# One more buffer for four attention tiles, and three small PSUM sums moved later, in a fused attention and two-layer kernel

## The chip, the cores and the metric

The kernel runs on one core of a Trainium2 chip. The metric is device microseconds of one execution. It was measured three times before the change; a fourth execution was taken with the hardware profiler, and all rows below are of that one.

## The reference

Attention over 4 batches, 8 heads, 576 positions, head size 64, with a causal mask and a bias from the running sums of `max(s, 0)`; the result, as 2304 tokens of 512, goes through two layers, `relu(x w_in)**2 w_out` and then `g w_out` with `g = h cos(h)`, `h = x w_in`, each with 2048 hidden columns.

```python
bias = -(cum[:, :, :, None] - cum[:, :, None, :])
scores = np.where(causal, -1e9, scale * q @ k.T + np.minimum(bias, 0.0))
attn = softmax(scores)
x = (attn @ v) as (2304, 512)
y = np.maximum(x @ w_in, 0.0) ** 2 @ w_out
h = y @ w2_in
out = (h * np.cos(h)) @ w2_out
```

## The kernel before, in words

Everything is written out by hand in one order for each engine; waits come from the tiles' dependencies. Work goes in two halves. In the first, attention for the next 256 tokens runs beside the first layer for the last 256: `step` (L1325) is called once for each attention job (at most 128 queries of one head), and each call also takes one or two slots of the first layer (`moe_slot`, L1285), 12 products each for one slice of 128 hidden columns, either into the slice (`g1`, L1148) or out of it (`g2`, L1189). In the second half only the second layer is left.

The first 16 heads run in a simple form, the other 80 units in a split form: a number is kept as a rounded part and a rest, and three products make one. For these, a call of `step` with job i does, in this order on TensorE: the first slot, the scores of job i (`emit_qk`, L539), further slots, the turning of a finished pair of heads (`turn`, L744), the product of job i-5 with v (`emit_pv`, L671). VectorE masks the scores of job i-1 (`emit_mask`, L573), rounds the weights p of job i-2 (`emit_split`, L629), evacuates finished heads (`evacuate`, L708), and makes the rests of the layer's slices (`grest`), of the turned x (`x_low`) and of the next head's q and k (`prep_low`, L406). ScalarE takes exponentials, squares and rounded parts (`prep_high`, L399, of q and k; `x_high`, L787, of x). SyncE issues nearly all DMAs in order: raw q and k of a head three ahead (`load_raw`, L239), v (`load_v`, L418) and the DMA transposes of p (`p_turn`, L624). GpSimd clears the ends of p's rows (L647) and issues the loads into k2.

The tiles in question lie in the pool `at` and rotate by tag. `raw` and `s` (the scores) have two buffers. `p` has two, and every third job takes the single buffer of tag `p3` instead, outside a stretch in which the weights are converted. `pt`, p turned, has three. Job i's `pt` is written at step i+2 and read at step i+5.

All small sums share one PSUM bank, `xps`: columns 0 to 255 take the turned x (L751), which `x_high` and `x_low` read; one column takes the sum of v's squares for a group of two heads (`v_sum`, L450), read by `v_scale` (L457, L461); 16 columns take the sums of the first layer's weight slices (`c_sums`, L834), read by `c_scales` (L841, L848).

There are 16 groups of v. `v_add` (L524) puts their parts on a list by step: square at the end of step t, sum at step t+1, scale at t+2. `v_late` runs at a step's end. A group with `v_wait` on the list has its sum at t+2, behind the first slot, and its scale at the end of the VectorE part of that step, behind the rounding of p, the slices' rests, the weights' conversion (`c_step`, L889) and `prep_low`:

```python
        slow = bool(vq) and any(f is v_wait for f, g in vq[0])
        if slow:
            v_sums()
```

In the kernel before only the third group has it. `c_step` squares the weights' slices one at a time (L861, ScalarE); `c_total` (L920) issues the sum for slices 0 to 11 and for 12 to 15 at the end of the step that squared the last of them. From the fourth block of tokens on the layer uses these scales.

Of the kernel before, what the change touches and what calls it, by code (L numbers as in the profile page):

```python
# [8 lines left out]
F32 = mybir.dt.float32  # L9
F32R = mybir.dt.float32r  # L10
F16 = mybir.dt.float16
# [7 lines left out]
B, H, S, D = 4, 8, 576, 64  # L19
# [4 lines left out]
NF = DFF // 128  # L24
# [18 lines left out]
SQ_A = 12  # L43
# [55 lines left out]
KQ = 832  # L99
# [32 lines left out]
def attention_moe_moe_kernel(  # L132
# [29 lines left out]
    at = at_stack.enter_context(tc.tile_pool(name="at", bufs=1, side="right"))  # L162
# [20 lines left out]
    wsc1, hs1, xm = sc1[:, 0:NF // 2], sc1[:, NF // 2:NF], sc1[:, NF:NF + 1]  # L183
    vsc = const.tile([128, B * H], F32, name="vsc")
    hd, vd, vown = {}, {}, {}
    cs = at.tile([128, S], F32, tag="s", bufs=2, name="cs")
    c8 = wp.tile([128, S], F32, tag=f"w{2 * NF - 8}", name="c8")
    nc.sync.dma_start(out=cs[0:32, 0:S], in_=s)
    wt, wst = {}, {}
# [34 lines left out]
    for x in range(H // 2):  # L224
        t = wp.tile([128, 2, 2 * BT], F32, tag=f"w{2 * NF - (2, 3, 4, 6)[x]}", name="early")
# [13 lines left out]
    def load_raw(n):  # L239
        nq, nl = _queries(heads[n]), heads[n][8]  # L240
        if n < H:
            return
        if n < EARLY:
            t = at.tile([128, KQ], F32, tag=("hi", "k2")[n % 2], bufs=2, name="early1")
            nc.sync.dma_start(out=t[0:64, 0:2 * BT], in_=qk[n, 0:64, 0:2 * BT])
            nc.sync.dma_start(out=t[64:66, 0:2 * BT], in_=c1_d[n - H])
            hd[n] = t
            return
        raw = at.tile([128, KQ], F32, tag="raw", bufs=2, name="raw")
        nc.sync.dma_start(out=raw[:, BT - nq:BT + nl], in_=qk[n, :, BT - nq:BT + nl])  # L250
        hd[n] = [None, None, raw]

# [114 lines left out]
    for x in range((XST + 1) // 2):  # L367
        t = wp.tile([128, 2, 512], F32, tag=f"w{2 * NF - 5 - x}", name="xst")
# [18 lines left out]
    lag1, wrest = [], []  # L387
# [136 lines left out]
    def v_add(gs, at, stored=True):  # L524

        for g, t in zip(gs, at):
            fs = []
            if g not in vs:
                fs, t = [(t, v_load)], t + 2
            late = g == gs[2]  # L530
            fs += [(t + 2, v_wait)] * late
            fs += [(t, v_square), (t + 1 + late, v_sum), (t + 2, v_scale), (t + 2, v_high), (t + 3, v_low)]
            for x, f in fs + [(t + 3, v_store)] * stored:
                vq.extend([] for _ in range(x + 1 - len(vq)))
                vq[x].append((f, g))
# [37 lines left out]
    def emit_mask(i):  # L573
        n, ti, q, r = jobs[i]
        j = jd[i]
        if _paired(heads[n]):
            if heads[n][2] % 2 == 0:
                return
            r = 128
        sb = at.tile([128, S + 2], F32, tag="s", bufs=2, name="sb")  # L580
        nb = sb[:, S:S + 2]
        for k, (p, c0, cn) in enumerate(j["ps"]):
            mo = 512 if _paired(heads[n]) and k else max(0, 384 - q + c0)
            nc.vector.tensor_tensor_reduce(  # L584
                out=sb[0:r, c0:c0 + cn], in0=p[0:r, 0:cn], in1=mask[0:r, mo:mo + cn],
                scale=-0.125, scalar=(3.0e38 if k == 0 else nb[0:r, 0:1]),
                op0=ALU.add, op1=ALU.min, accum_out=nb[0:r, k:k + 1],
            )
            yield
        j["sb"], j["nb"] = sb, nb[0:r, len(j["ps"]) - 1:len(j["ps"])]  # L590

    def p_tile(i):
        third = nw[2] >= 2 * NF and not wrest and i % 3 == 2 and (cdone[1] == 0 or 2 in w16 and 2 not in w32)
        return at.tile([128, 1280], F16, tag="p3" if third else "p", bufs=1 if third else 2, name="p")

    def emit_exp(i):
        n, ti, q, r = jobs[i]
# [31 lines left out]
    def emit_split(i):  # L629
        n, ti, q, r = jobs[i]  # L630
        j = jd[i]
        if _paired(heads[n]):
            if heads[n][2] % 2 == 0:
                return
            r = 128
        w, sb = j["w"], j["sb"]
        cw = 128 * ((w + 127) // 128)
        if n < EARLY:
            pp = j["ps"][0][0][:, BT:BT + cw]
            pt = at.tile([128, 640], F32, tag="pt", bufs=3, name="pt1")  # L640
            (nc.scalar.copy if ti else nc.vector.tensor_copy)(pt[:, 0:w], pp)
            j["pt"] = pt
            yield
            return
        p = p_tile(i)
        if cw > w:
            nc.gpsimd.memset(p[0:r, 0:2 * cw].rearrange("p (a c) -> p a c", a=2)[:, :, w:cw], 0.0)  # L647
        if 0 < cdone[1] and NF - 1 not in w16 and i % 2:
            nc.scalar.activation(out=p[0:r, 0:w], in_=sb[0:r, 0:w], func=ACTF.Copy, scale=PSC)  # L649
        else:  # L650
            nc.vector.tensor_scalar(  # L651
                out=p[0:r, 0:w], in0=sb[0:r, 0:w], scalar1=PSC, scalar2=None, op0=ALU.mult
            )
        yield
        nc.vector.scalar_tensor_tensor(  # L655
            out=p[0:r, cw:cw + w], in0=sb[0:r, 0:w], scalar=PSC, in1=p[0:r, 0:w],
            op0=ALU.mult, op1=ALU.subtract,
        )
        pt = at.tile([128, 1280], F16, tag="pt", bufs=3, name="pt")
        pt = pt[:, 0:2 * cw // 128 * r].rearrange("p (a r) -> p a r", r=r)  # L660
        turned.append((pt, p[0:r, 0:2 * cw]))
        if not last_block(i):
            p_turn()
        j["pt"] = pt
        if _paired(heads[n]):
            jd[i - 1]["pt"], j["pt"] = pt[:, :, 0:64], pt[:, :, 64:128]
        yield
# [161 lines left out]
    w16, cdone, csum, chigh, clow = {}, [0, 0, 0], [], [], []  # L829
# [57 lines left out]
    spare, w32 = [None], {}  # L887
# [29 lines left out]
            chigh.append((cdone[1], t))  # L917
            cdone[1] += 1

    def c_total():  # L920
        if cdone[0] == SQ_A and SQ_A not in csent:
            csent.append(SQ_A)
            c_sums(0, SQ_A)
        elif cdone[0] == NF and NF not in csent:
            csent.append(NF)
            c_sums(SQ_A, NF)

    csent = []
# [28 lines left out]
    nw = [2, 0, 0]  # L957
    stq = [(wp, 3)]
    p3 = [0]
# [314 lines left out]
    slots = []  # L1274
# [50 lines left out]
    def step(moe=0, bits=0, attn=True):  # L1325

        i = prog[0]
        held = len(xtq)
        prog[0] += attn
        if attn:  # L1330
            for j in stage(1, i - 2):
                emit_exp(j)
        x_high()
        if attn and job(i - 2):
            emit_turn(i - 2)
        if attn:
            heads_ahead(i, (next_, load_ext, 2))
        w_age()
        w_scales()
        n = moe_slot() if moe else None  # L1340
# [3 lines that stand above are left out]
        if attn:  # L1344
            heads_ahead(i, (nhigh, prep_high, 2))
        _weave(evacuate())
        y_evict()
        if not attn or g2done[0] < 2:
            rests()
        if xcq and xcq[-1][-1] and xcq[-1][0] == 1:  # L1350
            x_low()
        _weave(softmax_tail(i) if attn else None, w_step(bits), None if slow else v_early())
        x_low()
        rests()
        w_lows()
        if attn and job(i - 1) and jobs[i - 1][0] < EARLY:
            for j in stage(1, i - 1):
                emit_exp(j)
        act(n)
        if moe and slots and NF < slots[0][1] < (KC + 2) * NF:  # L1360
            c_step(slots[0][1])
        if attn:
            heads_ahead(i, (nlow, prep_low, 2))
        if slow:
            _weave(v_early())
        if not (attn and last_block(i)):
            y_store()
        if attn and job(i):
            emit_qk(i)
        if attn and last_block(i):  # L1370
            heads_ahead(i, (nraw, load_raw, 4))
        for _ in range(moe - 1):
            act(moe_slot())
            y_evict()
        w_sums()
        if attn:
            for j in stage(1, i - 1):
                emit_exp(j)
        behind = any(job(j) and _paired(heads[jobs[j][0]]) for j in (i - 6, i - 5))
        if attn and not behind:  # L1380
            values(i)
        turn(held if moe and i > last_job[0] + TURN_FROM else len(xtq))
        if not slow:
            v_sums()
        if attn:
            for j in stage(3, i - LAG[0]):
                if j > i - lag(j):
                    stages[3] -= 1
                    break
                emit_pv(j)  # L1390
        if attn and behind:
            values(i)
        if moe:
            c_total()
        p_turn()
        w_ahead()
        if attn:
            heads_ahead(i, (nraw, load_raw, 4))
        v_late()
        y_store()  # L1400
        if later and prog[0] >= later[0][0]:
            later.pop(0)[1]()
# [102 lines left out]
    while prog[0] < unit_done(0):  # L1505
        i = prog[0]
# [472 lines left out]
```

## Time and profile before

| | us |
|---|---|
| three runs | 964.85, 966.21, 966.48; median 966.21 |
| the profiled execution | 966.79 |
| its span, first to last instruction | 965.0 |
| TensorE busy | 933.0 (97%) |
| VectorE busy | 752.9 (78%) |
| ScalarE busy | 710.8 (74%) |
| GpSimd busy | 166.6 (17%) |
| granted TensorE clock | 1.00 of full speed all along |

TensorE is PE in the rows, its weight loads PEld, VectorE DVE, ScalarE ACT, GpSimd POOL; SPq is SyncE's queue. In a timeline row a bracket tells how long the engine was idle before the instruction and what ended that. In the table of waits the columns are: who waited, for whom, us in total, times, the longest. Attention ends at about 538 us of the span. A matmul's listed duration overlaps the next one's.

### The profile page before, as it was taken

How to read it: one execution, taken by the hardware profiler on the slowest of the kernel's cores; microseconds unless marked ns; L12 is line 12 of the kernel's file. 1: busy time of each engine (PE TensorE's matmuls, PEld its weight loads, DVE VectorE, ACT ScalarE, POOL GpSimd, SP SyncE). 2: the span in 40 equal slices, each digit the busy share in tenths (PEclk: the TensorE clock that was granted, in tenths of full speed). 3: DMA queues.
4: the chain of work that ended last, by engine and by line, in shares of the span. 5: the costliest groups of instructions: out<-in, count | busy, mean ns of one | idle time of the engine just before them, and what ended most of it. 6: DMA issues, size and time to landing. Idle time of an engine off the chain costs nothing.

```text
span 965.0 us, 21094 instructions
## 1 busy us (share of the span) xinstructions
PE 933.0 (97%) x7548; PEld 732.0 (76%) x7548; DVE 752.9 (78%) x1901; ACT 710.8 (74%) x1627; POOL 166.6 (17%) x306
## 2 busy tenths in 40 slices
PE   6999999989999999999999999999999999999998
PEld 5899998988998988889989986444544566666665
DVE  6899987789898866887997365799889877767654
ACT  6799887878897767676775686688767766656553
POOL 2000123222211222222330022421000000100101
PEclk9999999999999999999999999999999999999999
DMA  8984699657998987589998669310012111111101
GB/s 250 321 268 144 167 220 229 175 140 155 192 194 196 194 198 167 133 171 179 199 229 169 219 219 358 121 44 23 1 44 45 22 23 44 44 52 38 44 1 66
DMA packets 159225, 137.46 MB, mean 142 GB/s; under 512 B 109400, under 2 KB 132256, under 8 KB 159120
## 3 DMA queue, kind: packets, MB, share of 16 engines
q1 hardware_dynamic: 147664, 123.78, 50.4%
q0 software_dynamic: 11456, 12.34, 6.0%
q8 instruction: 59, 0.97, 0.4%
q14 instruction: 46, 0.38, 0.1%
HBM read 93.91 MB, written 15.83 MB: 114 GB/s over the span
## 4 chain that ended last, share of the span: by engine, by line
PE 63%; DVE 7%; ACT 2%; issue 2%; DMA 2%; SPq 0%; DVEq 0%; ACTq 0%
PE o L1663 18%; PE y L1196 12%; PE hp L1611 10%; PE hps L1164 10%; PE bank L1767 7%; PE qkp L566 3%; PE pvs L696 2%; DMA raw<-in_qk_dram 1%; DVE k L414 1%; DVE sb L584 1%; PE xps L751 1%; DVE gl L1186 1%; DMA vb<-v_d 0%; DVE p L651 0%; DVE wt L1680 0%
## 5 line engine op out<-in xcount | busy, mean ns | idle before, releaser
L1196 PE MATMUL y<-gh,wt 128*128 128x256 f32 x1152 | 237.3, 289 | 0.0
L1196 PEld LDWEIGHTS y<-gh,wt 128*128 128x128 f32 x1152 | 188.4, 190 | 1.2
L1663 PE MATMUL o<-wt,gh 128*128 128x512 f16 x576 | 171.3, 379 | 0.4 <-DVE wt L1680 0.4
L1196 PE MATMUL y<-gl,wt 128*128 128x256 f32 x576 | 162.7, 283 | 0.5 <-DVE gl L1186 0.5
L1164 PE MATMUL hps<-xh,w 128*128 128x256 f16 x1152 | 142.0, 273 | 2.7 <-ACT g L1176 2.6
L1164 PEld LDWEIGHTS <-w 128*128 128x128 f16 x1152 | 106.0, 98 | 17.8 <-issue 4.4
L1196 PEld LDWEIGHTS y<-gl,wt 128*128 128x128 f32 x576 | 109.8, 191 | 1.4 <-DVE gl L1186 0.9
L1663 PE MATMUL o<-wt,gl 128*128 128x512 f16 x288 | 109.2, 379 | 0.6 <-DVE gl L1649 0.6
L1611 PE MATMUL hp<-yh,wt 128*128 128x512 f16 (+1 forms) x384 | 104.5, 343 | 0.0
L1663 PEld LDWEIGHTS <-gh 128*128 128x128 f16 x576 | 56.3, 98 | 51.5 <-issue 0.6
L1176 ACT ACTIVATE g<-hps,sc 128x256 f32<-128x256 f32 x96 | 45.2, 470 | 63.0 <-PE hps L1164 60.8
L607 ACT ACTIVATE sb<-sb 128x128 f32<-128x128 f32 (+7 forms) x152 | 87.4, 575 | 5.0 <-DVE sb L584 4.6
L1611 PEld LDWEIGHTS <-wt 128*128 128x128 f16 x576 | 54.7, 98 | 47.7
L396 POOL DMA_DIRECT2D k<-ext_d x80 | 41.4, 518 | 265.5 <-PE qkp L566 156.7
L1767 PEld LDWEIGHTS <-wt 128*128 128x128 f16 x672 | 65.7, 98 | 21.5 <-issue 0.6
L1164 PE MATMUL hps<-xh,wt 128*128 128x256 f32 x384 | 80.3, 292 | 0.3 <-ACT g L1178 0.2
L1186 DVE TENSOR_TENSOR gl<-g,gh 128x256 fp32r<-128x256 f32 x144 | 60.4, 419 | 23.0 <-ACT gh L1180 14.9
L655 DVE SCALAR_TENSOR_TENSOR p<-sb,p 128x384 f16<-128x384 f32 (+3 forms) x120 | 66.3, 553 | 9.2 <-ACT p L649 6.0
L584 DVE CUSTOM_DVE_ANT_0 sb<-qkp,mask 128x128 f32<-128x128 f32 (+7 forms) x152 | 69.2, 455 | 4.8 <-PE qkp L551 3.9
L404 ACT CAST hi<-raw 128x704 fp32r<-128x704 f32 (+2 forms) x80 | 58.8, 735 | 12.9 <-DMA raw<-in_qk_dram 12.8
L1611 PE MATMUL hp<-yl,wt 128*128 128x512 f16 (+1 forms) x192 | 65.9, 343 | 0.0
L1164 PEld LDWEIGHTS hps<-xh,wt 128*128 128x128 f32 x384 | 63.5, 192 | 3.1 <-issue 1.5
(172 smaller groups left out, 2021.8 us busy)
## 6 DMA issues: line engine op xcount, KB each, us to landing
rw<-in_w_dram SPq DMA_DIRECT2D x64, 512.0 KB
raw<-in_qk_dram SPq DMA_DIRECT2D x48, 352.0 KB
yr<-y_d SPq DMA_DIRECT2D x17, 512.0 KB
raw<-in_qk_dram SPq DMA_DIRECT2D x16, 384.0 KB
v_d<-vt SPq DMA_DIRECT2D x16, 320.0 KB
vb<-v_d SPq DMA_DIRECT2D x32, 160.0 KB
vr<-in_v_dram POOLq DMA_DIRECT2D x15, 320.0 KB, 5.2
y_d<-yst SPq DMA_DIRECT2D x18, 256.0 KB
```

The lines of the kernel that those rows point to most:

```text
L396: nc.gpsimd.dma_start(out=hd[n][1][64:68, BT - nq:BT + nl], in_=ext_d[n, :, BT - nq:BT + nl])
L404: nc.scalar.copy(hi[:, BT - nq:BT + nk], raw[:, BT - nq:BT + nk])
L584: nc.vector.tensor_tensor_reduce(out=sb[0:r, c0:c0 + cn], in0=p[0:r, 0:cn], in1=mask[0:r, mo:mo + cn], scale=-0.125, scalar=(3.0e38 if k = ...
L607: nc.scalar.activation(out=sb[0:r, 0:w], in_=sb[0:r, 0:w], func=ACTF.Exp, scale=-1.0, bias=j["nb"], accum_out=z[0:r, ti, x:x + 1],)
L655: nc.vector.scalar_tensor_tensor(out=p[0:r, cw:cw + w], in0=sb[0:r, 0:w], scalar=PSC, in1=p[0:r, 0:w], op0=ALU.mult, op1=ALU.subtract,)
L1164: nc.tensor.matmul(hp, w[:, a, c * 128:(c + 1) * 128], (xh, xl)[e][:, c, :], start=(n == 0), stop=(n == 3 * KD - 1),)
L1176: nc.scalar.activation(out=g, in_=hp, func=ACTF.Relu, scale=hs1[:, f // 2:f // 2 + 1])
L1186: nc.vector.tensor_tensor(out=gl, in0=g, in1=gh, op=ALU.subtract)
L1196: nc.tensor.matmul(yps[k][d // 2][:, d % 2, :], w[:, a, d * 128:(d + 1) * 128], (gh, gl)[e], start=(f == 0 and n == 0 and d % 2 == 0), sto ...
L1611: nc.tensor.matmul(hp, chunk_of(w, a, c), (yh, yl)[e][:, c, :], start=(m == 0), stop=(m == 3 * KD - 1),)
L1663: nc.tensor.matmul(ops[j][a], (gh, gl)[e][:, a * 128:(a + 1) * 128], w[:, x, :], start=(first and m == 0), stop=(last and m == 2),)
L1767: nc.tensor.matmul(bank[b][:, 0:HB], w[:, a, wx, c * 128:(c + 1) * 128], y_side(j, yx, e, c), start=(start and n == 0), stop=(n == 5), ski ...
```

## The change

The four tags `s` (also used once by `cs` at the start), `raw`, `p` and `pt` get one buffer more, and `p3` is taken by every fourth job. All groups of v but the first get the later sum and scale. `c_total` is told the next slot's slice number and holds each of its two sums back until that number has passed a bound, which is two steps later than before.

```diff
-        raw = at.tile([128, KQ], F32, tag="raw", bufs=2, name="raw")
+        raw = at.tile([128, KQ], F32, tag="raw", bufs=3, name="raw")
...
-            late = g == gs[2]
+            late = g != gs[0]
             fs += [(t + 2, v_wait)] * late
             fs += [(t, v_square), (t + 1 + late, v_sum), (t + 2, v_scale), (t + 2, v_high), (t + 3, v_low)]
...
-        sb = at.tile([128, S + 2], F32, tag="s", bufs=2, name="sb")
+        sb = at.tile([128, S + 2], F32, tag="s", bufs=3, name="sb")
...
-        third = nw[2] >= 2 * NF and not wrest and i % 3 == 2 and (cdone[1] == 0 or 2 in w16 and 2 not in w32)
-        return at.tile([128, 1280], F16, tag="p3" if third else "p", bufs=1 if third else 2, name="p")
+        third = nw[2] >= 2 * NF and not wrest and i % 4 == 3 and (cdone[1] == 0 or 2 in w16 and 2 not in w32)
+        return at.tile([128, 1280], F16, tag="p3" if third else "p", bufs=1 if third else 3, name="p")
...
-        pt = at.tile([128, 1280], F16, tag="pt", bufs=3, name="pt")
+        pt = at.tile([128, 1280], F16, tag="pt", bufs=4, name="pt")
...
-    def c_total():
-        if cdone[0] == SQ_A and SQ_A not in csent:
+    def c_total(t):
+        if cdone[0] == SQ_A and SQ_A not in csent and t > NF + SQ_A + 3:
             csent.append(SQ_A)
             c_sums(0, SQ_A)
-        elif cdone[0] == NF and NF not in csent:
+        elif cdone[0] == NF and NF not in csent and t > 2 * NF + (NF - SQ_A) + 4:
...
-        if moe:
-            c_total()
+        if moe and slots:
+            c_total(slots[0][1])
```

The tag `pt` goes from three to four for the first 16 heads' `pt1` as well, and `cs` gets `bufs=3`.

## Rows read from the trace of the kernel before

**Rows 1.** The page, part 1: busy time, share of the span, instructions of each engine.

```profile
PE 933.0 (97%) x7548; PEld 732.0 (76%) x7548; DVE 752.9 (78%) x1901; ACT 710.8 (74%) x1627; POOL 166.6 (17%) x306
```

**Rows 2.** Windows: PE, PEld, DVE, ACT, POOL busy, granted clock, DMA share, GB/s.

```profile
192.00:240.00 48.00, 44.23 (x401) 40.98 (x401) 42.33 (x146) 39.89 (x108) 12.65 (x31) 1.00 0.64 149
240.00:336.00 96.00, 95.49 (x1000) 88.43 (x1000) 84.19 (x220) 80.60 (x191) 21.42 (x45) 1.00 0.94 194
...
456.00:528.00 72.00, 69.93 (x773) 64.83 (x771) 63.93 (x187) 50.09 (x115) 18.15 (x45) 1.00 1.04 207
```

**Rows 3.** Waits of PE, 96 to 240 us.

```profile
PE xps L835 <- ACT wj L861: 1.6, 1, 1.6
PE pvs L696 <- DVE xp L736: 1.4, 1, 1.4
PE xps L751 <- DVE vsc L461: 0.9, 1, 0.9
...
PE xps L751 <- DVE yss L848: 0.8, 1, 0.8
PE qkp L566 <- DVE k L414: 0.7, 2, 0.4
PE qkp L566 <- DVE hi L411: 0.5, 1, 0.5
```

**Rows 4.** Waits of PE, 240 to 530 us.

```profile
PE qkp L566 <- DVE sb L584: 2.6, 7, 0.6
PE pvs L696 <- DMA vb<-v_d: 1.2, 2, 0.7
PE xps L452 <- DVE xh L824: 0.9, 1, 0.9
PE xps L751 <- DVE xp L736: 0.5, 1, 0.5
```

**Rows 5.** Waits of SyncE's queue, whole span.

```profile
SPq L627 <- PE pvs L696: 40.2, 43, 2.1
SPq L250 <- DVE k L414: 39.2, 20, 8.5
```

**Rows 6.** Timeline of SyncE's queue: p's transpose, then a load of raw.

```profile
331.88 1.27 SPq L627 DMA_TRANSPOSE pt<-p  x1
...
333.87 0.37 SPq L250 DMA_DIRECT2D raw<-in_qk_dram  x1
```

**Rows 7.** Timeline of ACT: the rounding of that load.

```profile
340.34 0.78 ACT L404 CAST hi<-raw 128x704 fp32r<-128x704 f32 x1 [3.57 <-DMA raw<-in_qk_dram]
```

**Rows 8.** Windows, as rows 2, of four us within that wait.

```profile
336.00:340.00 4.00, 3.79 (x41) 3.41 (x40) 1.48 (x6) 0.74 (x2) 1.25 (x3) 1.00 1.30 160
```

**Rows 9.** Waits of DVE, whole span.

```profile
DVE p L651 <- POOL p L647: 5.3, 7, 1.0
```

**Rows 10.** Timeline of PE and DVE at 203 us: a turning, a scale, the step's prep_low.

```profile
203.54 0.48 PE L751 MATMUL xps<-ident,xp 128*128 128x128 f32 x2
...
203.10 0.15 DVE L461 TENSOR_SCALAR vsc<-xps 128x2 int32<-128x2 int32 x1
...
205.81 0.42 DVE L414 TENSOR_TENSOR k<-raw,hi 64x256 fp32r<-64x256 f32 x1
```

**Rows 11.** Timeline of PE and DVE at 187 us: a turning, the step's prep_low.

```profile
187.54 0.27 PE L751 MATMUL xps<-ident,xp 64*128 64x64 f32 x1
...
188.67 0.42 DVE L414 TENSOR_TENSOR k<-raw,hi 64x256 fp32r<-64x256 f32 x1
```

**Rows 12.** Timeline of PE and DVE at 236 us: a turning, the step's last slice rest.

```profile
235.88 0.53 PE L751 MATMUL xps<-ident,xp 128*128 128x128 f32 x2 [0.86 <-DVE vsc L461]
...
236.49 0.42 DVE L1186 TENSOR_TENSOR gl<-g,gh 128x256 fp32r<-128x256 f32 x1
```

**Rows 13.** Timeline of PE and ACT at 283 us: scores behind a slot, x_high.

```profile
282.49 0.39 PE L566 MATMUL qkp<-hi 128*128 128x512 f32 x1
...
283.65 0.46 ACT L801 ACTIVATE xh<-xps,yss 128x256 f16<-128x256 f32 x1
```

More of the change, by code (lines that the diff above doesn't have):

```diff
@@ L185, in attention_moe_moe_kernel @@
     hd, vd, vown = {}, {}, {}
-    cs = at.tile([128, S], F32, tag="s", bufs=2, name="cs")
+    cs = at.tile([128, S], F32, tag="s", bufs=3, name="cs")
     c8 = wp.tile([128, S], F32, tag=f"w{2 * NF - 8}", name="c8")
@@ L639, in emit_split @@
             pp = j["ps"][0][0][:, BT:BT + cw]
-            pt = at.tile([128, 640], F32, tag="pt", bufs=3, name="pt1")
+            pt = at.tile([128, 640], F32, tag="pt", bufs=4, name="pt1")
             (nc.scalar.copy if ti else nc.vector.tensor_copy)(pt[:, 0:w], pp)
```

## The prediction, made before the changed kernel ran

> **What bounds the kernel now.** I read the page's busy times first: TensorE is busy 97% of the span [rows 1], so what an edit of this kind can win is TensorE's idle time, some 32 us, and only the part of it that the edit reaches. Then the windows [rows 2]. In all of them the granted clock is 1.00, so no clock is lost or to be won back. Between 240 and 336 us TensorE is busy 95.49 of 96 us: there nothing waits, and whatever makes it wait is paid in full. Between 192 and 240 it is idle 3.8 us while VectorE is busy 42.3 and ScalarE 39.9 of 48: while the weights are being converted these two set the pace. Between 456 and 528 VectorE is busy 63.9 of 72 us.
>
> The table of TensorE's waits then says what each idle time ended on [rows 3, 4]. The groups shown lie between 96 and 530 us, where the change works, and hold 11.1 us: a sum of weights' squares behind ScalarE (1.6), v's product behind VectorE's xp (1.4), turnings behind a scale of v (0.9) and behind the weights' scales (0.8), scores behind q and k's rests (0.7 and 0.5), scores behind masks (2.6 in seven), v's product behind a load (1.2), one sum of v's squares behind x_low (0.9), and a turning behind xp (0.5). No row of either table has TensorE waiting for a transposed p: a fourth buffer for it can help only through others.
>
> **Raw and pt.** No instruction is added. SyncE's queue waits 40.2 us in 43 pieces for v's product to free pt before it can issue a transpose, and 39.2 us in 20 for k's rest to free raw [rows 5]; both disappear, and the queue then waits for the rounding of p, in the same step. All that stands behind these in the queue goes out sooner: loads of v, raw, v's stores, weights. The place where it shows: a transpose goes out at 331.88, the load of raw behind it at 333.87 [rows 6], and ScalarE stands still 3.57 us for it until 340.34 [rows 7]; behind that come scores that wait. What the load gains is at most the wait before that transpose, and one such wait is at most 2.1 us [rows 5]. The rests cost 0.7 + 0.5 [rows 3]; lower bound nothing, upper 1.2 plus the one mask wait of 0.6 that follows the stall at 340. I take 1.2 in all: most of the first, half the second. For the loads of v (1.2 in two, [rows 4]) I take 0.4: the queue ahead of them is mostly issuing, not waiting; bounds 0 and 1.2. For the other six mask waits, 2.0 us, I take 0.9: ScalarE's waits for raw go, but VectorE is nearly full in that window [rows 2]; bounds 0 and 2.0.
>
> **s and p.** A score buffer comes free when VectorE has rounded p, an earlier instruction of the engine that then writes the buffer: nothing to win, nothing to lose. For p, VectorE waits 5.3 us in seven for GpSimd's clearing [rows 9], and that clearing waits for the transpose that frees the buffer. With a reuse distance of four jobs instead of three (three instead of two during the conversion) these go, but VectorE's time counts only where TensorE waits for it: the turning at 236 us, 0.9 [rows 3, 12]. I take 0.5, between 0 and 0.9. The space costs no time by itself; the attention pool grows, and the second layer's tiles then lie over other tiles of it. What they wait for may change; the cover is that these loads are issued some steps ahead of their first use. I cost it at nothing, with one load's wait, 0.6 either way [rows 4], in the range.
>
> **The two sums of weights.** The second one stops TensorE for 1.6 us, as it is issued right behind ScalarE's square [rows 3]. Two steps later it does not wait. But TensorE's next stop, at 214.6 us, 1.4 us for xp [rows 3], is set by VectorE, and VectorE and ScalarE are full in between: what TensorE no longer loses at the first it waits at the second. The turning of the same step also gets a wait of its own (below). I take 0; bounds 1.6 won and 1.3 lost. The first sum ends with a turning 0.8 us late behind the scales made from it; these move behind that turning, and a scale of v just before them stays: 0.4 of 0.8.
>
> **The fourteen moved sums and scales of v.** Nothing is added: one weight load and one product of one column move from a step's end to behind the next first slot, and two VectorE instructions of 0.15 us [rows 10] move from among the masks to behind `prep_low`. One gain is direct: the 0.9 us for x_low [rows 4] goes, as the sum now comes before the next x_low. Against it, all of this is in the bank into which turned x is written. Two waits can arise.
>
> First, a turning in the same step must wait for the scale, which now comes after the rests. I followed the fourteen groups through the timeline; a turning in the scale's own step, close to it, is there in three. At 187 us prep_low ends at 189.09, the scale 0.15 later, and the turning stood at 187.54: 1.7 us [rows 11]. At 203 us prep_low ends at 206.23, so the turning moves from 203.54 to 206.38, 2.8 us [rows 10]; but the 1.6 us for the weights' sum behind it are gone, and of the 1.3 left the 1.4 at 214.6 us takes all. At 236 us, with no prep_low in that step, the slice's rest ends at 236.91: 1.2 us [rows 12]. Queued behind the waiting turning are v's product of that step and the next slot; behind those, ScalarE's squares.
>
> Second, where a turning was in the step before, the sum must wait for x_high. At 283 us the first slot ends where the scores begin, at 282.49, and x_high ends at 284.11: 1.6 us [rows 13], in the stretch that has no idle time.
>
> The bound against is 1.7 + 1.2 + 1.6 = 4.5 us. I take 0.9 of the first, since TensorE comes later to the stop at 214.6, 0.4 of the second, since VectorE comes there earlier by p's waits, and 1.1 of the third, since 0.5 of it is idle at the next turning behind xp [rows 4]: 2.4.
>
> **The sum.** Won: 1.2 + 0.4 + 0.9 + 0.5 + 0.4 + 0.9 = 4.3. Lost: 2.4. Net 1.9. Of the profiled execution's 966.79 us (span 965.0), that leaves 964.9; the median of the runs is 0.6 lower, so the forecast for the median is 966.2 - 1.9 = 964.3. A measurement of this kernel can tell about 0.2%, 1.9 us, from no change; the forecast stands on that line, on the faster side if the masks' waits go a little further than half.
>
> **Rival 1: the shared bank decides, slower.** The moved scales land behind the turnings and the moved sum behind x_high, and the waits are paid in full, 4.5 us, while of the gains only those on the same bank and p's stay: 0.9 + 0.4 + 0.5. That gives 966.2 + 2.7 = 968.9. It decides once VectorE reaches the end of its step later than TensorE reaches the turning by more than the 1.4 us that is idle at 214.6 anyway. For it: VectorE's 42.3 of 48 us, and that all four places are computed from instructions that stand there. Against it: VectorE loses its own waits for p, and TensorE pays only what is not idle later. The Trainium skill, page PSUM — Partial Sum Buffer, section on bank collisions, has a rule that speaks against putting such a sum there: two engines must be kept apart by bank and quadrant, not by address, reads against reads included. By that rule each of the four places costs its whole wait, and the time is this rival's. The trace agrees as far as it shows it: the sum, in a column of its own, waited 0.9 us for a reader of other columns [rows 4].
>
> **Rival 2: the early loads win nothing, same.** At 336 to 340 us, within ScalarE's long wait, the DMA engines' share is 1.30 [rows 8]; a load that is issued one or two us sooner may land when it did. Then raw's 1.2, the masks' 0.9 and the loads' 0.4 fall away; 1.8 won against 2.4 lost: 966.8. For it: that share, and that the load took 6.5 us from 333.87 to 340.34 [rows 6, 7]. Against it: over 240 to 336 the share is 0.94 [rows 2], so sooner is not always into a full engine. The Trainium skill, page DMA: Bandwidth & Descriptors, section Issuing engines are not separate DMA queues, says that DMAs of all queues end up on the same 16 engines and interleave. By that an earlier issue moves a place in one line and no more, and the time is this rival's; the trace's shares do not decide it. That the buffers do nothing at all, because no one waits for a transposed p, is the same case with p's 0.5 gone.
>
> **How the numbers follow.** Faster, the forecast with what the masks add: 0.43. Rival 2 and everything near it, within 1.9 us: 0.35. Rival 1: 0.22. The range runs from gains near their bounds (raw 1.8, p 0.9, the direct 0.9, scales 0.8, masks 2.0, loads 1.2, less 2.4, so 5.2 won, 0.6 for the space: 960.4) to rival 1's 968.9.
>
> **What would show it.** Right: SyncE's waits for v's product and for k's rest gone from its table; ScalarE's wait at 340 us shorter by over a microsecond; the wait for x_low gone; the weights' sum without a wait. Wrong: turnings that wait for a scale of v with more than 3 us in all, or a sum of v's squares that waits for x_high: rival 1. Unchanged waits for raw: rival 2. Waits over a microsecond that name a tile of neither kind, in the second layer's first 60 us, would mean that I missed what the shifted space does.

## The result, and the profile after

| | before | after |
|---|---|---|
| median, us (4 runs each) | 966.35 | 973.34 |
| the profiled execution, us | 966.79 | 973.08 |
| its span, us | 965.0 | 971.3 |

The ratio is 1.0064, with an interval from 1.0048 to 1.0079. By the ratio the change makes the kernel slower by 6.2 us (4.6 to 7.6); the two medians lie 7.0 us apart. 973.34 is above the range (up to 968.9).

Part 1 of the page after the change; it answers to [rows 1].

```profile
PE 936.8 (96%) x7548; PEld 736.7 (76%) x7548; DVE 754.1 (78%) x1901; ACT 711.0 (73%) x1627; POOL 167.0 (17%) x306
```

The same 7548 products are listed with 936.8 us in place of 933.0, and TensorE's idle time, span less busy, goes from 32.0 to 34.5. Of 6.3 us more, only 2.5 are idle time; the rest is listed as busy time, with no product added, which alone does not say why. The windows, as in [rows 2], say where to look.

```profile
192.00:240.00 48.00, 45.30 (x378) 41.87 (x377) 39.39 (x133) 36.83 (x102) 11.79 (x28) 0.95 0.57 135
240.00:336.00 96.00, 92.96 (x955) 86.10 (x955) 82.31 (x219) 79.71 (x188) 18.69 (x42) 0.98 0.84 185
456.00:528.00 72.00, 69.67 (x763) 64.43 (x762) 64.61 (x188) 51.08 (x117) 19.48 (x48) 1.00 0.93 201
```

The granted clock, 1.00 in all three before, is 0.95 and 0.98 in the first two. The third window is nearly as it was. VectorE evacuates the same block of y at 179.38 before and 177.68 after, the next at 246.99 and 254.06, the one at attention's end at 547.76 and 554.05; from there to the end the two kernels run 6.3 us apart. So all is lost between 178 and 254 us, 8.8 us, with 1.3 in the next block; 2.6 are won from 313 to 436.

TensorE's waits after the change: 96 to 240 us, then 240 to 530, answering to [rows 3, 4].

```profile
PE xps L751 <- DVE vsc L461: 5.6, 2, 3.1
PE xps L751 <- DVE xp L736: 1.0, 1, 1.0
PE xps L835 <- DVE vsc L461: 0.5, 1, 0.5
PE xps L452 <- ACT x L807: 0.4, 1, 0.4
PE qkp L566 <- DVE k L414: 0.4, 1, 0.4
...
PE qkp L566 <- DVE hi L411: 0.2, 1, 0.2
```

```profile
PE qkp L566 <- DVE sb L584: 2.9, 7, 0.6
PE xps L751 <- DVE vsc L461: 1.6, 1, 1.6
PE xps L452 <- ACT xh L801: 1.5, 1, 1.5
PE pvs L696 <- DMA vb<-v_d: 0.8, 2, 0.6
```

Gone are the weights' sum behind the last square (1.6), the turning behind the weights' scales (0.8), v's product and a turning behind xp (1.4, 0.5) and the sum behind x_low (0.9). Against that stand three turnings behind a scale of v, 7.3 us in all (the third waited 0.9 before), a sum behind x_high, 1.5, and two small new waits, of 0.5 and 0.4. The timeline shows the three and the sum; it answers to [rows 10 to 13].

```profile
189.02 0.42 DVE L414 TENSOR_TENSOR k<-raw,hi 64x256 fp32r<-64x256 f32 x1
...
189.36 0.15 DVE L461 TENSOR_SCALAR vsc<-xps 128x2 int32<-128x2 int32 x1
...
189.56 0.27 PE L751 MATMUL xps<-ident,xp 64*128 64x64 f32 x1 [3.05 <-DVE vsc L461]
...
209.29 0.42 DVE L414 TENSOR_TENSOR k<-raw,hi 64x256 fp32r<-64x256 f32 x1
209.63 0.14 DVE L461 TENSOR_SCALAR vsc<-xps 128x2 int32<-128x2 int32 x1
...
209.83 0.53 PE L751 MATMUL xps<-ident,xp 128*128 128x128 f32 x2 [2.57 <-DVE vsc L461]
...
240.96 0.41 DVE L1186 TENSOR_TENSOR gl<-g,gh 128x256 fp32r<-128x256 f32 x1
241.30 0.14 DVE L461 TENSOR_SCALAR vsc<-xps 128x2 int32<-128x2 int32 x1
...
241.50 0.76 PE L751 MATMUL xps<-ident,xp 128*128 128x128 f32 x2 [1.64 <-DVE vsc L461]
...
290.81 0.45 ACT L801 ACTIVATE xh<-xps,yss 128x256 f16<-128x256 f32 x1
291.31 0.16 PE L452 MATMUL xps<-ss,ones 128*128 128x1 bf16 x1 [1.54 <-ACT xh L801]
```

Each turning starts right behind a scale that stands behind `prep_low`'s last instruction, or, at 241, behind the slice's rest. What follows each is seen in windows around them (columns as in [rows 2]).

```profile
186.00:190.00 4.00, 0.95 (x11) 0.68 (x11) 3.48 (x17) 3.94 (x13) 0.20 (x1) 1.00 0.52 126
190.00:194.00 4.00, 4.00 (x43) 3.90 (x39) 2.73 (x7) 0.94 (x3) 0.00 (x0) 0.57 0.43 102
207.00:210.00 3.00, 0.43 (x3) 0.20 (x2) 2.64 (x9) 2.75 (x8) 0.00 (x0) 1.00 0.33 87
210.00:214.00 4.00, 4.00 (x26) 3.60 (x26) 2.71 (x10) 2.36 (x6) 0.00 (x0) 0.60 0.46 127
240.00:242.00 2.00, 0.50 (x2) 0.28 (x2) 1.97 (x8) 1.51 (x5) 1.40 (x4) 0.89 0.82 233
242.00:246.00 4.00, 4.00 (x37) 3.77 (x38) 3.74 (x9) 2.05 (x5) 0.00 (x0) 0.63 0.55 110
```

After each wait TensorE is busy all the time, but at a granted clock of 0.57 to 0.63 over four us. The clock's records put it at 0.5, the lower of its two levels (1.2 in place of 2.4 GHz), for 3.41 us from 190.35, 210.83 and 241.55. While TensorE sets the pace, 3.41 us at half speed cost at most 1.7 us, three times 5.1. In the profiled execution before, the records have 0.5 nowhere but from 965.53 us, behind the last instruction. One such stretch lowers an execution's mean granted clock by 0.0018. All four executions after the change have a mean of 0.992 to 0.996; of the 95 of the kernel before that were taken beside the experiments, 22 have 0.997 or less, so it loses the clock in mid-run now and then too.

Behind the first wait lies another new one, on VectorE. The timelines of VectorE and of SyncE's queue, after the change:

```profile
179.67 0.42 DVE L1186 TENSOR_TENSOR gl<-g,gh 128x256 fp32r<-128x256 f32 x1
183.50 0.69 DVE L871 TENSOR_TENSOR w<-wt 128x512 f32<-128x512 f32 x1 [3.42 <-DMA pt<-p]
```

```profile
179.83 1.34 SPq L627 DMA_TRANSPOSE pt<-p  x1
```

L871 adds the two parts of the first weight slice that is to be converted and writes them into `w32`, a tile of the tag `p3` (L868). It waits until the p of the last job in `p3` has been turned. On the gaining side SyncE's queue and VectorE, whole span, answer to [rows 5, 9]:

```profile
SPq L627 <- PE pvs L696: 14.4, 16, 1.6
...
SPq L250 <- DVE k L414: 6.5, 2, 6.2
```

```profile
DVE p L651 <- POOL p L647: 3.8, 5, 1.0
```

ScalarE's waits for raw between 96 and 540 us fall from 12.8 us in nine to 2.6 in two; the 3.57 us of [rows 7] are gone.

### The profile page after: what moved, and what is told of

Same layout as the page of the kernel before. It is cut to its first block, busy times and chain, and to the rows that moved or that the text cites. A ratio compares the mean times of both kernels' runs of the same rounds, so it can differ in the third digit from the quotient of the medians.

```text
span 971.3 us, 20980 instructions
## 1 busy us (share of the span) xinstructions
PE 936.8 (96%) x7548; PEld 736.7 (76%) x7548; DVE 754.1 (78%) x1901; ACT 711.0 (73%) x1627; POOL 167.0 (17%) x306
## 4 chain that ended last, share of the span: by engine, by line
PE 59%; DVE 6%; ACT 2%; issue 2%; DMA 1%; POOL 0%; DVEq 0%; ACTq 0%
PE o L1663 18%; PE hp L1611 10%; PE y L1196 10%; PE hps L1164 9%; PE bank L1767 7%; PE qkp L566 2%; PE pvs L696 2%; DVE k L414 1%; DMA rw<-in_w_dram 1%; DVE sb L584 1%; PE xps L751 0%; DVE gl L1186 0%; DMA vb<-v_d 0%; DVE p L651 0%; DMA yr<-y_d 0%
## 5 line engine op out<-in xcount | busy, mean ns | idle before, releaser
L1164 PE MATMUL hps<-xh,w 128*128 128x256 f16 x1152 | 142.0, 273 | 3.0 <-ACT g L1176 3.0
L1164 PEld LDWEIGHTS <-w 128*128 128x128 f16 x1152 | 106.0, 98 | 18.1 <-issue 4.8
L1164 PE MATMUL hps<-xh,wt 128*128 128x256 f32 x384 | 83.3, 299 | 0.3 <-ACT g L1178 0.2
L1164 PEld LDWEIGHTS hps<-xh,wt 128*128 128x128 f32 x384 | 66.1, 200 | 1.6 <-ACT g L1178 1.0
L1649 DVE TENSOR_TENSOR gl<-a,gh 128x512 f16<-128x512 f32 (+1 forms) x80 | 52.3, 669 | 16.0 <-ACT gh L1642 15.5
```

Source lines behind the costliest of these rows:

```text
L1164: nc.tensor.matmul(hp, w[:, a, c * 128:(c + 1) * 128], (xh, xl)[e][:, c, :], start=(n == 0), stop=(n == 3 * KD - 1),)
L1649: nc.vector.tensor_tensor(out=gl, in0=a, in1=gh, op=ALU.subtract)
```

## The experiments

The theory at the start: because of the scales' new place three turnings wait, and each wait is followed by a stretch at half clock; the rest of the change gains a little. Ratios are to the kernel before, run on the same chip, with 95% intervals; a us figure behind one is its distance from 1, times 966.

**The parts, one by one.** First the change without its moved sums and scales.

```diff
-            late = g != gs[0]
+            late = g == gs[2]
```

> The changed kernel with only the fourteen moved sums and scales of v put back. Theory (the moved scales make three turnings wait, 7.3 us, a sum waits 1.5 us for x_high, and the granted clock stands at half for 3.41 us behind each of the three long waits): 962 to 965 us, ratio 0.996 to 0.999, no wait of a turning for a scale over 1 us, granted clock 1.00 at 186 to 246 us. Rival A (the buffers or the shifted space cost the time): still over 970. Rival B (the delayed sums of the weights cost it): still over 970, with the long waits gone or not.

Measured: 964.75 us, ratio 0.9988 (0.9978 to 0.9998). Then each of the three parts in the kernel before, alone: the line above the other way round, the four tags with the modulus of `p3`, and `c_total`.

> The kernel before with only the fourteen moved sums and scales of v. Theory: three turnings wait 6 to 8 us in all for scales, three stretches at half clock, 973 to 978 us, that is more than the whole change costs, as the buffers are not there to give 3 or 4 us back. Rival A and rival B (buffers, space or the weights' sums cost the time): 965 to 968, no half clock. Rival C (the waits arise only because the buffers let VectorE and SyncE run in another order): no turning waits over 1 us for a scale.

Measured: 972.7 us, 1.0064 (1.0051 to 1.0076), or 6.2 us. TensorE's waits in it, whole span:

```profile
PE xps L751 <- DVE vsc L461: 7.4, 4, 2.6
```

The waits are there without any of the buffers, and with them the whole loss, so rivals A, B and C fall. Only one of the waits, of 2.56 us, was followed by a stretch at half clock in the profiled execution, where I expected three. The third turning, in the place where the whole change lost its clock, kept it here:

```profile
241.24 0.53 PE L751 MATMUL xps<-ident,xp 128*128 128x128 f32 x2 [1.63 <-DVE vsc L461]
```

```profile
242.00:246.00 4.00, 4.00 (x47) 3.82 (x43) 3.66 (x8) 3.48 (x9) 0.00 (x0) 1.00 0.75 90
```

After nearly the same wait, 1.63 us and 1.64, 47 products are listed in these four us at 1.00, where 37 stood at 0.63. The part costs no less than the whole change, but I had expected it to cost 3 or 4 us more. That pointed at the buffers.

> The kernel before with only the four tags' additional buffers. Theory: 962 to 965 us, with SyncE's wait for v's product under 20 us and its wait for k's rest gone; the gain where ScalarE stood at 340 us. Prediction's rival 2 (loads that go out sooner land when they did): 966 to 967. Rival A (the buffers cost): over 968.

Measured: 965.69 us, 0.9998 (0.9987 to 1.0009): no gain, though SyncE's wait for v's product is 13.7 us. My theory missed here. The profiled execution is the slowest of the twelve, 969.57 us, and has two stretches at half clock, from 166.41 and 190.30 us.

> The kernel before with only the weights' two sums delayed. Theory: TensorE's wait of 1.6 us for the last square is gone and most of it comes back at the next stop, 965 to 967 us. Rival B (the later scales of the weights hold up the layer): over 968 with a new wait over 1 us that names these scales. The prediction's bounds: 1.6 won, 1.3 lost.

Measured: 965.0 us, 0.9990 (0.9981 to 0.9999): a gain of 1.0 us. The three parts alone give 6.2 - 0.2 - 1.0 = 5.0 us, inside the interval of the whole, 4.6 to 7.6.

**Place of the scale, or of the sum.** The whole change, with the two scale instructions among the masks again:

```diff
-        _weave(softmax_tail(i) if attn else None, w_step(bits), None if slow else v_early())
+        _weave(softmax_tail(i) if attn else None, w_step(bits), v_early())
...
-        if slow:
-            _weave(v_early())
```

> The changed kernel with the sums of v's squares left where the change put them, behind the first slot, but the two scale instructions back among the masks instead of behind the rests of q and k. Theory (the scale's place makes the turnings wait): no turning waits over 0.5 us for a scale, no half clock at 186 to 246 us, the sum's wait of 1.5 us for x_high stays; 961 to 965 us. Rival D (the sum's place, ahead of scores and turning, is what costs): 969 or more, with VectorE waiting for the sum, or the sum waiting for x_high, in place of the turnings.

Measured: 966.58 us, 1.0009 (0.9998 to 1.0020). The waits from 96 to 540 us:

```profile
PE xps L751 <- DVE vsc L461: 1.9, 2, 1.1
PE xps L452 <- ACT xh L801: 1.5, 1, 1.5
```

Some 5.3 of the 6.2 us are gone, so rival D falls and the scale's place is what costs. The time stayed above my 961 to 965: a turning still waited 1.1 us at 188 us, and half clock followed.

**Three groups, or all fourteen.**

```diff
-            late = g != gs[0]
+            late = gs.index(g) not in (0, 6, 7, 8)
```

> The changed kernel with three of the fourteen groups put back, the seventh, eighth and ninth, whose turnings waited 3.05, 2.57 and 1.64 us. Theory: nearly all of the loss goes, 962 to 966 us; the other eleven cost the wait of 1.5 us for x_high and little else; at 186 us the wait that the kernel without moved sums had (1.9 us and one stretch at half clock) may come back, which is where 966 comes from. Rival E (the loss is spread over all fourteen groups): 969 to 972.

Measured: 966.99 us, 1.0009 (0.9997 to 1.0022). Three groups hold nearly all; rival E falls. It is 1 us above my range, and the wait that I thought might return did (96 to 540 us):

```profile
PE xps L452 <- ACT x L807: 1.9, 1, 1.9
PE xps L452 <- ACT xh L801: 1.5, 1, 1.5
```

**One group alone**, in the kernel before: `late = gs.index(g) in (2, 8)`.

> The kernel before with one more group moved, the ninth alone (turning at 236 us). Theory with the clock: TensorE waits about 1.6 us in place of 0.9 at that turning, and behind it 3.41 us at half clock cost 1.7 us more: 967.5 to 969.5 us. Rival F (the wait counts by its length alone, the clock costs nothing that shows): 966.5 to 967.3.

Measured: 967.8 us, 1.0017 (1.0004 to 1.0030). The turning waited 1.6 us, but the clock stayed full behind it in the profiled execution; a stretch at half clock stood at 160 us, behind 1.24 us of idle time in a part that the edit does not reach. Neither theory is shown by the times, as the interval reaches into both ranges.

**More work in place of the waits.** The whole change, and in the three steps the products of the scores repeated:

```diff
-            for m, kk in ((hi, 128), (k2, 68)):
+            for m, kk in ((hi, 128), (k2, 68)) * (1 + again[0] * (not two)):
...
         slow = bool(vq) and any(f is v_wait for f, g in vq[0])
+        again[0] = sum({6: 8, 7: 6, 8: 4}.get(vg.index(g), 0) for f, g in vq[0] if f is v_wait) if slow else 0
```

> The changed kernel with more work: in the three steps whose turning waits for a scale, the pair of products that makes the job's scores is repeated 8, 6 and 4 times into the same bank, 0.37 us a pair, so that TensorE computes while it would have waited. Theory with the clock: the turnings still start when their scale is there, but the granted clock stays 1.00 behind them, and the time falls by about three times 1.7 us: 967 to 969.5 us. Rival F (the clock costs nothing that shows; only the waits do): 972.5 to 974, or slower by what the products overrun.

Measured: 968.99 us, 1.0040 (1.0026 to 1.0055), span 966.8. The stretches behind the waits, in windows:

```profile
190.00:194.00 4.00, 4.00 (x56) 3.79 (x56) 2.95 (x10) 2.31 (x8) 0.52 (x1) 1.00 0.48 112
...
210.00:214.00 4.00, 4.00 (x40) 3.72 (x39) 3.20 (x10) 3.40 (x11) 1.27 (x3) 1.00 0.49 123
...
242.00:246.00 4.00, 4.00 (x34) 3.80 (x34) 3.76 (x11) 3.26 (x9) 0.46 (x1) 1.00 0.79 187
```

With 36 more products the clock is 1.00 in all three, 56 products are listed from 190 to 194 us in place of 43, and the profiled span is 4.5 us shorter. By the ratios it is 2.3 us, and the two intervals, 1.0026 to 1.0055 and 1.0048 to 1.0079, overlap.

**The buffers' lost gain.** The wait of 1.9 us that came back stands in the first experiment's timeline too. VectorE's, then TensorE's rows, and a window behind them:

```profile
183.61 0.69 DVE L871 TENSOR_TENSOR w<-wt 128x512 f32<-128x512 f32 x1 [3.54 <-DMA pt<-p]
```

```profile
186.01 0.16 PE L452 MATMUL xps<-ss,ones 128*128 128x1 bf16 x1 [1.93 <-ACT x L807]
```

```profile
186.00:190.00 4.00, 3.98 (x31) 3.64 (x31) 3.44 (x17) 3.94 (x13) 0.20 (x1) 0.57 0.49 121
```

VectorE stands 3.54 us for a transpose, ScalarE then for VectorE's masks, the sum of v's squares for ScalarE's x, and the clock halves. All six profiles with the new modulus so far have this wait of VectorE, 3.4 to 3.6 us; the four without it (the kernel before among them) do not. The condition `i % 3 == 2` gave `p3` last to job 53 before the conversion began; `i % 4 == 3` gives it to job 55, whose p is turned right before the first converted slice needs the buffer. So four runs keep job 55 out:

```diff
-        third = nw[2] >= 2 * NF and not wrest and i % 4 == 3 and
+        third = nw[2] >= 2 * NF and not wrest and i % 4 == 3 and i != 55 and
```

> The changed kernel with the sums and scales of v put back, as in the first experiment, and with job 55 kept out of the tag p3. Theory P (taking p3 by every fourth job gives it to job 55, whose transpose the first converted slice of the weights, w32 in the same buffer, must then await: VectorE stands 3.5 us, the sum of v's squares behind it waits 1.9 us, and the clock halves): VectorE's wait, the sum's wait and the half clock at 186 us gone, 960.5 to 962.5 us, ratio about 0.995. Rival G (the stall at 183 us is absorbed by the stops that follow; the buffers have nothing more to give): 964 to 965.5.

Measured: 963.37 us, 0.9965 (0.9952 to 0.9978). Its VectorE at the same place:

```profile
178.65 0.42 DVE L1186 TENSOR_TENSOR gl<-g,gh 128x256 fp32r<-128x256 f32 x1
178.98 0.69 DVE L871 TENSOR_TENSOR w<-wt 128x512 f32<-128x512 f32 x1
```

The wait is gone, and so are the sum's and the half clock. The median is 0.9 above my range, the ratio is 2.2 us better than with job 55 in `p3`.

> The kernel before with only the additional buffers, and job 55 kept out of the tag p3. Theory P: the buffers then give what the prediction named for them, 2 to 4 us: 962 to 964. Rival G or the prediction's rival 2 (the loads win nothing): 965 to 966.5, no better than with job 55 in p3.

Measured: 963.73 us, 0.9966 (0.9953 to 0.9979). The buffers alone, with one job kept out of one tag, win 3.3 us (2.0 to 4.5) where they won 0.2. Rival G and the prediction's rival 2 fall.

> The whole change with job 55 kept out of the tag p3. Theory P: VectorE's wait of 3.4 us at 183.5 gone, the first of the three turnings waits about 2 us in place of 3.05, the other two stay: 969.5 to 972 us. Rival G: 973 as before. Rival H (that wait alone causes the first stretch at half clock and more): under 969.

Measured: 969.25 us, 1.0027 (1.0013 to 1.0040). The waits from 96 to 540 us, and the windows behind the second and third turning:

```profile
PE xps L751 <- DVE vsc L461: 5.8, 3, 2.6
```

```profile
209.00:213.00 4.00, 4.00 (x25) 3.80 (x24) 3.33 (x9) 2.73 (x9) 1.26 (x3) 0.58 0.27 79
240.00:244.00 4.00, 4.00 (x35) 3.90 (x33) 3.41 (x7) 2.05 (x6) 0.00 (x0) 0.61 0.53 106
```

The first turning waits 1.63 us, without half clock behind it; the others wait 2.56 and 1.64, with it. The time is a little below what I expected.

> The change with three things put right: job 55 kept out of p3, the scales back among the masks, and the eleventh group, whose sum waited 1.5 us for x_high, put back. Theory with P: no wait over 1.5 us between 96 and 540 us, no half clock, 959.5 to 962.5 us, faster than both kernels. Rival D (the sums' later place costs by itself): more than the kernel with all sums put back and job 55 kept out, by over 1.5 us.

Measured: 963.81 us, 0.9967 (0.9955 to 0.9980), as with all sums put back. No stretch at half clock before the end; the median is 1.3 us above my range. Sums behind the first slot are harmless where their scale is early and no x_high stands before them. They also win nothing.

**The clock or the wait**, once more, without the wait for `p3`, with job 55 kept out and 6, 10 and 6 repeated pairs:

> The whole change, job 55 kept out of p3, and the waits of the three turnings filled: the pair of products of the job's scores is repeated 6, 10 and 6 times in these steps. It stands against the same kernel without the filling, whose ratio to before is 1.0027 (1.0013 to 1.0040), with two stretches at half clock in its profile. Theory with the clock: the turnings still start when the scale is there, no half clock, 3 us less, ratio 0.999 to 1.000. Rival F (the clock costs nothing that shows): 1.0027 or more.

Measured: 967.23 us, 1.0012 (0.9999 to 1.0026). The waits from 96 to 540 us, under this file's line numbers, and the windows as above:

```profile
PE xps L753 <- DVE vsc L462: 0.4, 2, 0.2
```

```profile
209.00:213.00 4.00, 4.00 (x42) 3.72 (x40) 2.75 (x8) 3.41 (x11) 1.27 (x3) 1.00 0.45 123
240.00:244.00 4.00, 4.00 (x44) 3.82 (x43) 3.90 (x10) 3.15 (x8) 1.06 (x4) 1.00 0.80 162
```

44 more products make the kernel no slower, and by the middle of the ratios 1.5 us faster, half of the 3 that I expected. The profile shows the clock at 1.00 and 42 products where 25 stood. In both pairs the intervals of the ratios overlap, so the times alone do not say what the clock costs.

The traces do. The first products into the layer's slices (L1164) come in the same order in all kernels, so the time from one of them to a later one can be compared. The table has how much longer than in the kernel before it takes around each turning; an h marks a stretch at half clock behind the wait.

| us more than before | 183.88 to 192.42 | 200.24 to 214.68 | 231.07 to 240.31 |
|---|---|---|---|
| whole change | 5.2 h | 1.3 h | 2.3 h |
| whole change, filled | 3.7 | -0.2 | 0.9 |
| whole, without job 55 | 1.7 | 1.3 h | 2.4 h |
| whole, without job 55, filled | 1.7 | -0.2 | 1.5 |
| sums and scales alone | 2.1 | 1.2 h | 0.9 |

At the third turning the wait is 1.64 us in the two kernels with an h, and 1.63 in the sums alone, which have no added product; with the ninth group alone it is 1.62, also without half clock, and the extra time 0.9. So the half clock itself costs 1.5 us there. Filling saves 1.5 at each of the other two. (The 1.5 in the fourth row is no half clock: there the products repeated outlast the scale, which has ended at 238.46, until 239.20 us.) In the profiled execution of the whole change the clock thus takes some 4.4 of the 8.8 us that are lost between 178 and 254, and the wait for `p3` takes 2.0, the 3.7 less the 1.7. What the clock costs on average over executions is not shown as well: without job 55, the five executions with a mean clock of 0.998 have a median of 967.28 us and the seven with less 970.31, but of the six with the sums alone the one with 0.998 is the slowest.

## Why the prediction was wrong

**The side.** Rival 1 had the mechanism, with its four places, and a chance of 0.22; I forecast the other. Its price, 968.9, was too low as well: it has neither the clock nor the wait for `p3`. The Trainium skill's page PSUM — Partial Sum Buffer, section PSUM bank collisions raise a hardware error, has the rule to keep engines apart by bank and quadrant, not by address. The trace agrees: in all four places TensorE waited for a reader of other columns of the bank, 3.05, 2.57, 1.64 and 1.54 us. What a place then costs is another number, which the next paragraph takes from the trace.

**The four places: sized nearly rightly, netted too far.** I worked out 1.7, 2.8, 1.2 and 1.6 us, 7.3 in all; the measured waits are 8.8, or 7.4 without the wait for `p3`, and 0.9 of the third was there before. I then kept 0.9, 0, 0.4 and 1.1, 2.4 in all. By the table, without half clock and `p3`, the first costs 1.7, the second wins 0.2, the third costs 0.9; around the sum behind x_high, from 279.06 to 294.45 us, the whole change is 1.1 longer. That makes 3.4. The netting of the second came out: the weights' sum no longer waits, and the stop at 214.6, which no longer occurs, pays the rest. But the prediction drew on its 1.4 us twice, for the second place and again for 0.8 of the first, which was paid whole. At the third it took 0.8 off for VectorE's earlier end, and the trace shows 0.3. Together the netting was 1.0 us short.

**The clock: no term at all.** This is the step that failed by most. "In all of them the granted clock is 1.00, so no clock is lost or to be won back" reads the kernel before and was carried over to a kernel with longer waits. Three waits of 1.64 to 3.05 us were each followed by 3.41 us at half clock, 4.4 us in all by the table, where the sum has nothing. The Trainium skill, page TensorE: Matmul & The Clock Gate, section HAM oscillation — how this bites in real kernels, says that waits in a stream of products drop the engine to the lower clock, and that the restart is paid again each time; the trace agrees for the three waits, with 0.57 to 0.63 in the windows behind them, but not for the 1.54 us at x_high, behind which the clock stayed at 1.00.

**p: the lower bound was wrong.** "I take 0.5, between 0 and 0.9" counted the reuse distance and not which job holds `p3` last. The modulus moves its last holder from job 53 to job 55, and VectorE stops 3.4 us at the first converted slice, of which 2.0 reach TensorE in the whole change; at the same place the kernel with the sums put back is 3.5 us later than before, with the half clock behind its wait. I had read the condition on `cdone` as a stretch of time, and did not look up who next takes the tag.

**The buffers otherwise: right.** Raw, the loads, the masks and p were taken as 3.0 us; with job 55 out, 3.3 (2.0 to 4.5) was measured. Not by every row, though: the waits for masks did not shrink (2.6 to 2.9 us), the loads of v gave 0.4 as said, q and k's rests 0.6 of 1.2, and the sum's wait for x_low falls to 0.2 with the buffers alone, so that 0.9 was not the moved sum's to win. SyncE's waits fell by two thirds and five sixths and did not go. The attention pool's larger space cost nothing: 6.3 us apart at 554 us and at the end.

**The weights' sums.** I took 0 for the second and 0.4 for the first; alone, both give 1.0 us (0.1 to 1.8).

By the same steps with what was measured in the ratios: sums and scales 6.2 lost, `p3` some 3.1 lost (the buffers' 3.3 that became 0.2), the buffers 3.3 won, the weights' sums 1.0 won: 5.0, against 6.2 (4.6 to 7.6). In the profiled execution, which ends 6.3 us later where 1.9 less was forecast, the clock is 4.4, `p3` 2.0 and the netting 1.0 of the difference of 8.2; the gains fell short by the other 0.8.

## What to carry to other kernels

Before a small instruction is moved behind a longer stretch of its engine's step, look up who waits for the bank it reads; where the engine with the bound waits longer than before, add a term for the clock that it may lose behind that wait, and count each idle time elsewhere against the waits only once. When a rotation is changed, follow each buffer to whoever takes it next, not only to the next tile of the same kind. Here the better version is the buffers without that hand-over, with the weights' later sums and without the moved sums of v: 963.37 us, 0.9965 (0.9952 to 0.9978), faster than both kernels.

## What was not expected of the hardware

The fall of the clock did not follow from one wait's length alone. Between 96 and 540 us of these profiles, single idle times of 2.56 (twice), 2.57 and 3.05 us were all followed by 3.41 us at half clock. Of those from 1.5 to 2 us, 1.64 (twice), 1.78, 1.93 and 1.94 were; 1.99, 1.63 (twice), 1.62 and a number around 1.55 were not. Of shorter ones, one of 1.12 us, 1.7 us after one of 0.46, was, and one of 1.24 and one of 0.95, each with one of 0.37 right behind it; others of 1.1 to 1.5 were not. Of the first 42 us, where TensorE is idle for a good part at the start, the records of the clock say nothing: in all fifteen traces they begin later.

The kernel with such waits also varied more on its chip: twelve runs of the whole change without job 55 in `p3` lie between 966.28 and 972.23 us, seventeen of the kernel before between 963.84 and 968.01. And a single profile is no finer than about a us: in that of the kernel with one more group moved, the evacuation of y that stood at 110.75 us comes at 111.71, though its edit reaches nothing before 230 us.
